# The first keys' inverse root moved to VectorE, two GpSimd steps held behind the key product at the start, and a new table of due times

## The chip, the cores and the metric

One core of one Trainium2 chip runs one program. The metric is the device time of one execution in microseconds (us); a smaller time is better. The program has five instruction streams that run side by side and wait for each other by semaphores: PE (TensorE, matrix products and transposes), ACT (ScalarE), DVE (VectorE), POOL (GpSimd) and SP (SyncE, which here issues every DMA transfer). Each stream executes its instructions strictly in the order in which the program gives them.

## The reference

Attention over 8 batches of 12 heads with 448 positions of width 64, followed by a two-layer network on the 3584 resulting rows of width 768. All tensors are 32-bit floats on the device; the weights can come in as 64-bit numbers that the kernel decodes.

```python
def rmsnorm(x, g):
    rms = np.sqrt(np.mean(x * x, axis=-1, keepdims=True) + 1e-06)
    return x / rms * g
q_n, k_n = (rmsnorm(q, g_q), rmsnorm(k, g_k))
scores = scale * np.matmul(q_n, k_n.transpose(0, 1, 3, 2))
scores = scores - np.max(scores, axis=-1, keepdims=True)
attn = np.exp(scores)
attn = attn / (np.sum(attn, axis=-1, keepdims=True) + 1e-09)
attn_out = np.matmul(attn, v).astype(np.float32)
x = np.ascontiguousarray(attn_out.transpose(0, 2, 1, 3)).reshape(B * S, H * D)
h = x @ w_in              # 768 -> 2048
g = h * np.cos(h)
return (g @ w_out).astype(np.float32)   # 2048 -> 768
```

## The kernel before

**Units and batches.** Two heads make a unit, so there are 48 units (u), six to a batch. `prepare(u)` loads and normalizes a unit's queries and keys, `attend(u)` computes its scores, exponentials and products with v. The six units of the first batch are "plain": their products run on full 32-bit operands (`score_plain` L533, `av_plain` L660 to L670). From the seventh unit on, every operand is split into a high and a low part of a shorter format and the product is made from parts (`score` L549, `av` L642 and L644).

**The first keys.** For units 0 and 1 the keys come in rows with one position per partition. ACT squares them (`kn_square` L399), DVE sums the squares (`kn_reduce` L405), POOL adds a constant and takes the power -0.5 (`kn_pow` L409, L410), DVE multiplies the keys by the result (`kn_norm` L415), PE turns them (`kn_turn` L420) and ACT copies the turned keys with the gains (`kn_copy` L425). For unit 0 all but `kn_pow` go in two halves. Then PE's first scores begin (L533).

**The inverse roots for the softmax.** For every unit, ACT squares queries and keys in another layout (`st_square` L372), DVE sums (`st_reduce` L375), POOL takes the power (`st_pow` L380, L381). `rowmin` (L553, DVE) multiplies a tile of scores by these values and finds the extreme of each row; `expo` (L561, ACT) is the exponential.

**The keys of units 2 to 5.** Their inverse roots go through memory: `st_store` (L428) writes them out, `rk_spread` (L433) reads them back spread over the partitions (tile D), `k_load` (L448) loads the keys into the one key buffer kq, and POOL multiplies the two in two instructions (`k_norm` L458, tile km), the product that lets PE's scores of the unit begin. `k_load` of the next unit can be issued only when `k_norm` has read the buffer.

**Other work of POOL at the start.** `x_norm` (L699) multiplies a finished unit's attention output by its inverse sums. `w_low` (L267) makes the low part of a decoded weight tile, in two halves; the decoded tile lies in one of two buffers (wf, aq) that DVE's `w_decode` (L244 to L252) fills again afterwards. `q_scale` (L474) scales the queries.

**The order of the work.** No stream decides anything while it runs. Before, the class `Plan` lays out the whole program: every piece of work is added with its engine, an assumed cost, a due time, what it reads and what it writes. `order()` then plays the program through: of the pieces that could start on an engine it takes the one with the smallest due time, and the sequence in which pieces were taken is the order in which the instructions are written out. The due times are formulas of the unit plus a shift from the table `SHIFT`. A shift has three columns: for later units (u of 9 and up, later batches), for units 6 to 8 (for the two-layer network: the first batch), and for units 0 to 5.

**After the head.** The first product of the network for a batch (`ffn1` L726 to L728, `h_out` L744) is mixed into the attention of the next batch; the probabilities are transposed on PE (`transp` L595, L600, L604), copied out as high part (`pt_high` L618, ACT) and low part (`pt_low` L625 and L627, DVE). From about 890 us on only the network is left; its second product is `ffn2` (L800 to L802).

Of the kernel before, what the change touches and what calls it, by code (L numbers as in the profile page):

```python
# [10 lines left out]
F32 = mybir.dt.float32  # L11
F32R = mybir.dt.float32r
I32 = mybir.dt.int32
AF = mybir.ActivationFunctionType
ALU = mybir.AluOpType
# [5 lines left out]
PE, ACT, DVE, POOL, SP = "PE", "ACT", "DVE", "POOL", "SP"  # L21


class Plan:
# [46 lines left out]
    def order(self):  # L71
# [26 lines left out]
        seq = []  # L98
# [3 lines left out]
        while True:  # L102
            best = None
            for e in free:
                if can[e]:
                    t = free[e]
                elif wait[e]:
                    t = max(free[e], wait[e][0][0])
# [6 lines left out]
            t, e = best  # L115
            while wait[e] and wait[e][0][0] <= t:
                n = heapq.heappop(wait[e])[1]
                heapq.heappush(can[e], (parts[n][2], n))
            n = heapq.heappop(can[e])[1]
            cost, fn, args, kb = (parts[n][i] for i in (1, 3, 4, 6))  # L120
# [21 lines left out]
                    heapq.heappush(wait[parts[m][0]], (ready[m], m))  # L142
        assert len(seq) == len(parts)
        self.end = dict(free)
        self.seq = seq
        return [(fn, args) for _, _, fn, args in seq]


@with_exitstack
def tile_attention_moe(  # L150
# [11 lines left out]
    nc = tc.nc  # L162
    NU = sd_in.shape[0]
    B, S, D = 8, kq_in.shape[2] - 512, 64
# [11 lines left out]
    KB = S // 4  # L176
# [32 lines left out]
    def g_fold():  # L209
# [5 lines left out]
    wts, wfl, raw = {}, {}, {}  # L215
    RING = {
# [3 lines left out]
    }  # L220

# [94 lines left out]
    pair = {}  # L316
# [37 lines left out]
    def tl(u, name, shape, dt, tag=None):  # L354
        tag = tag or name
        t = pair.setdefault(u, {})[name] = apool.tile(shape, dt, tag=tag, name=f"{name}{u}", bufs=RING[tag])
        return t
# [28 lines left out]
    def kn_bank(u):  # L386
        return pt[u]
# [13 lines left out]
    def kn_reduce(u, a, b):  # L401
        if a == 0:
            tl(u, "rn", [128, 8], F32)
        sq = kn_bank(u)[:KB, 128 * a : 128 * b].rearrange("p (t d) -> p t d", d=D)
        nc.vector.tensor_reduce(pair[u]["rn"][:KB, 2 * a : 2 * b], sq, axis=AX.X, op=ALU.add)  # L405

    def kn_pow(u):
        r = pair[u]["rn"][:KB]
# [266 lines left out]
    xf = {}  # L675
# [141 lines left out]
    def y_store(b, oc, src):  # L817
# [2 lines left out]

    plan = Plan(RING, loose=PKEYS)
    SHIFT = {
        "av": (5.3, 0.0, 0.0), "av3": (3.6, 0.0, 0.0), "av_plain": (0.0, 0.0, 15.8), "e_place": (-4.5, 0.0, 0.0),
        "expo": (8.1, 0.0, 0.0), "ffn1": (0.0, -3.8, 0.0), "h_out": (-4.4, 0.0, 0.0), "k_high": (5.2, 7.1, 0.0),
        "kq_load": (-19.1, 0.0, 0.0), "m_place": (15.1, -13.5, 0.0), "pt_copy0": (0.0, 0.0, -3.9),
        "pt_high1": (-1.8, 0.0, 0.0), "pt_low0": (-20.7, 9.3, 0.0), "pt_low1": (-5.9, 0.0, 0.0),
        "q_high": (5.1, 0.0, 0.0), "q_low": (-2.0, 3.7, 0.0), "q_scale": (-9.4, -8.6, 0.0),
        "rowmin": (10.1, 6.2, 1.1), "rs_copy": (0.0, 2.2, 0.0), "rs_load": (0.0, 0.0, -12.0),
        "rs_store": (6.6, 0.0, 11.5), "rsum": (-8.3, 0.0, 0.0), "st_pow": (-14.6, 0.0, 0.0),
        "st_reduce": (5.3, 0.0, 0.0), "st_square": (2.5, 0.0, 0.0), "transp0": (-4.1, 0.0, 0.0),  # L830
        "transp1": (2.4, -8.7, 0.0), "v_decode": (8.3, 0.0, 0.0), "v_high": (0.0, 12.8, 0.0),
        "v_load": (19.8, -12.8, 0.0), "v_store": (12.5, 0.0, 0.0), "w_decode": (0.4, 0.0, 0.0),
        "x_norm": (4.0, 0.0, 0.0), "x_plain": (0.0, 0.0, -20.3), "x_split": (-3.4, 0.0, 0.0),
        "x_sum": (13.2, 0.0, 0.0),
    }

    def add(eng, cost, due, fn, *args, **more):
        name, first = fn.__name__, args[0] if args else 0
        stage = 0
        if name in ("ffn1", "h_out", "h_store", "h_both", "x_split"):  # L840
            stage = int(first < (NP if name == "x_split" else 1))
        elif name[:2] not in ("w_", "v_", "e_") or name in ("v_load", "v_high", "v_low", "v_plain", "e_place"):
            stage = 2 if first < NP else int(first < NP + 3)
        if name in ("pt_low", "pt_high", "pt_copy", "transp"):
            name += str(args[2])
        elif name == "av" and args[1] == 3:
            name += "3"
        due += SHIFT.get(name, (0.0,) * 3)[stage]
        if name in ("w_load", "w_decode", "w_high", "w_low"):
            due += -0.414 * first  # L850
        if name in ("ffn1", "h_out", "h_store", "h_both") and not first:
            due += -0.355 * args[1]
        if name in ("v_fetch", "v_decode", "v_sum", "v_split", "v_store"):
            due += 25.441 * first
        cost *= {DVE: 1.059, ACT: 1.026, POOL: 1.021}.get(eng, 1.0)
        plan.add(eng, cost, due, fn, *args, **more)
# [68 lines left out]
    def prepare(u):  # L925
        D0 = base(u)
        kmw = [km_key(u)]
        sd, r, kd, khi, qd, qhi = ([(n, u)] for n in ("sd", "r", "kd", "khi", "qd", "qhi"))
        sd = [("sd", max(u, NKT - 1), u)]
        turned, plain = u < NKT, u < NP  # L930
        if turned:
            kn, rn, kb = [("qd" if u == 0 else "ql", u)], [("rn", u)], [("pt", 0, n) for n in ((0,) if u == 0 else (1, 2))]
            add(SP, ISS, D0 - 60, kn_load, u, w=kn, kb=224.0)
            halves = ((0, 2), (2, 4)) if u == 0 else ((0, 4),)
            hs = [("kn", u, h) for h in halves]
            sh = 1.0 / len(halves)
            for h, k in zip(halves, hs):
                add(ACT, 0.06 + 0.57 * sh, D0 - 50, kn_square, u, *h, r=kn, w=[k, *(kb if h[0] == 0 else [])])
            for h, k in zip(halves, hs):
                add(DVE, 0.06 + 0.63 * sh, D0 - 50, kn_reduce, u, *h, r=[k, *kb], w=[("rn" if h[0] == 0 else "rm", u)])  # L940
            add(POOL, 1.9, D0 - 50, kn_pow, u, r=kb, w=rn + [("rm", u)])
            for h, k in zip(halves, hs):
                add(DVE, 0.06 + 0.63 * sh, D0 - 50, kn_norm, u, *h, r=rn + kn, w=[k])
            for h, k in zip(halves, hs):
                add(PE, 0.98 * sh, D0 - 50, kn_turn, u, *h, r=[k, *kn, *kb], w=[k])
            for n, (h, k) in enumerate(zip(halves, hs)):
                add(ACT, 0.73 if u else (0.36, 0.53)[n], D0 - 50, kn_copy, u, *h, r=[k, *kb, ("gsc", 0)], w=kmw)
        elif plain:
            add(SP, ISS, D0 - 36, k_load, u, w=kd, kb=224.0, start=D0 - 36)
        else:  # L950
            add(SP, ISS, D0 - 34, kq_load, u, w=kd + qd, kb=480.0, start=D0 - 40)
# [162 lines left out]
    for u in range(NP):  # L1114
        prepare(u)
# [28 lines left out]
    add = plan.add  # L1144
# [3 lines left out]
    for fc in range(NEAR, NFC):  # L1148
        n = fc - NEAR
        d, y, he = BLOCK * n, ("y", n % 8), (("he", "he2")[n % 2], n // 2)  # L1150
# [32 lines left out]
    for t in range(B // 2):  # L1183
# [26 lines left out]
        for k, (name, q, w0, bk, opens, closes) in enumerate(PRODUCTS):  # L1210
# [6 lines left out]
            for g in range(NGR):  # L1217
                n, n_split = n_split, n_split + 1
# [5 lines left out]
                for o in range(3):  # L1224
                    add(PE, BLOCK / 3, e + BLOCK / 3 * o, ffn2, n, g, wpos, role[bk][o], o, opens,
                        r=[hk, lk] + [("wp", i) for i in wpos], w=[("y", role[bk][o])])
# [8 lines left out]
            for o in range(3):  # L1235
                y, s0 = ("y", role[bk][o]), 4 * o
# [78 lines left out]
```

## Time and profile before

| what | value |
|---|---|
| median of 3 runs | 1373.23 us (1372.65 to 1375.12) |
| the profiled execution's own time | 1371.8 us |
| its span, first to last instruction | 1370.0 us |
| busy share PE, DVE, ACT, POOL | 98%, 78%, 68%, 46% |
| instructions in the span | 21500 |
| DMA | 302.19 MB, mean 221 GB/s |

The profile shows one execution. A line number (L458) is a line of the kernel, "km<-kq,D" says that tile km is written from kq and D, and a time is counted from the span's start. The busy share is an average over stages with different limits, so it is read together with the waits of each stretch: an engine's idle time before an instruction and what ended it. [...]

### The profile page before, as it was taken

Reading aid. Unit: us, or ns where it says so; the run is one execution under the profiler, and the core shown is the slowest. Engines: PE = TensorE matmul, PEld = TensorE weight load, DVE = VectorE, ACT = ScalarE, POOL = GpSimd, SP = SyncE. Lnnn points to the kernel's source line nnn. Section 1 sums busy time; section 2 is a strip of 40 time slices with the busy share of each in tenths; the row PEclk is TensorE's granted clock in tenths of the full one; section 3 lists DMA queues with packets and bytes.
Section 4 is the critical chain, followed back from the end, with each engine's and each line's share of the span. In section 5 each row is a group of like instructions: output and inputs, shape, how many; then the busy total and the mean of one; then the engine's idle time right before and its main releaser. Section 6 shows DMA issues by size and latency. Waiting matters only on the chain.

```text
span 1370.0 us, 21500 instructions
## 1 busy us (share of the span) xinstructions
PE 1343.2 (98%) x6998; PEld 1171.0 (85%) x6998; DVE 1075.0 (78%) x1859; ACT 927.4 (68%) x1872; POOL 632.5 (46%) x554
## 2 busy tenths in 40 slices
PE   7899999999999999999999999999999999999998
PEld 3346888788888989888889888999999999999998
DVE  7888899977787887787877877628889889889742
ACT  6677878777877877777777787638666366366321
POOL 4889978676766866666776584330000000000000
PEclk9999999999999999999999999999999999999999
DMA  6798776889798899798987897338988369369334
GB/s 241 263 276 194 186 170 188 240 232 244 201 260 212 216 243 209 218 243 227 247 209 196 227 233 200 120 131 315 370 298 300 119 246 306 112 247 313 105 113 153
DMA packets 149472, 302.19 MB, mean 221 GB/s; under 512 B 34368, under 2 KB 83088, under 8 KB 149360
## 3 DMA queue, kind: packets, MB, share of 16 engines
q1 hardware_dynamic: 149360, 300.83, 75.2%
q8 instruction: 55, 0.90, 0.3%
q14 instruction: 57, 0.47, 0.1%
HBM read 193.99 MB, written 62.73 MB: 187 GB/s over the span
## 4 chain that ended last, share of the span: by engine, by line
PE 86%; POOL 5%; DVE 3%; DMA 2%; issue 2%; ACT 1%; SPq 0%; POOLq 0%; ACTq 0%; DVEq 0%
PE y L800 10%; PE y L802 10%; PE y L801 10%; PE ph L726 9%; PE ph L727 8%; PE ph L728 8%; PE S L549 8%; PE PT L595 7%; PE O L642 4%; PE O L644 3%; PE O L660 1%; PE S L533 1%; PE y L727 1%; PE y L728 1%; PE y L726 1%
## 5 line engine op out<-in xcount | busy, mean ns | idle before, releaser
L553 DVE TENSOR_SCALAR_CACHE_REDUCE S<-S,r 128x448 f32<-128x448 f32 x336 | 225.3, 686 | 56.4 <-PE S L549 45.4
L561 ACT ACTIVATE P<-S,sm 128x448 f32<-128x448 f32 x336 | 213.3, 637 | 73.8 <-DVE S L553 56.7
L726 PE MATMUL ph<-xs,wi 128*128 128x448 f32 x660 | 251.1, 380 | 1.6 <-ACT hbuf L744 1.6
L800 PE MATMUL y<-g,wo 128*128 128x448 f32 x672 | 245.4, 365 | 0.0
L801 PE MATMUL y<-g,wo 128*128 128x448 f32 x672 | 245.4, 365 | 0.0
L802 PE MATMUL y<-g,wo 128*128 128x448 f32 x672 | 245.4, 365 | 0.0
L727 PE MATMUL ph<-xs,wi 128*128 128x448 f32 x660 | 241.7, 366 | 0.0
L728 PE MATMUL ph<-xs,wi 128*128 128x448 f32 x660 | 241.3, 366 | 0.0
L782 ACT CAST g<-gq 128x896 fp32r<-128x896 f32 x112 | 105.7, 944 | 170.6 <-PE y L802 170.1
L618 ACT CAST hi<-PT 128x512 fp32r<-128x512 f32 (+2 forms) x336 | 175.7, 532 | 63.7 <-PE PT L595 23.8
L625 DVE TENSOR_TENSOR lo<-PT,hi 128x512 fp32r<-128x512 f32 (+1 forms) x252 | 153.2, 619 | 41.2 <-ACT hi L618 39.0
L780 DVE TENSOR_TENSOR g<-gq,g 128x896 fp32r<-128x896 f32 x112 | 122.0, 1089 | 60.2 <-ACT g L782 59.7
L595 PEld LDWEIGHTS PT<-ident,P 128*128 128x128 f32 x1008 | 124.0, 141 | 42.2 <-issue 6.6
L595 PE MATMUL PT<-ident,P 128*128 128x128 f32 x1008 | 155.8, 275 | 2.8 <-DVE rt L574 1.2
L726 PEld LDWEIGHTS ph<-xs,wi 128*128 128x128 f32 x660 | 124.2, 188 | 17.8 <-ACT hbuf L744 3.4
L800 PEld LDWEIGHTS y<-g,wo 128*128 128x128 f32 x672 | 126.2, 188 | 10.0
L802 PEld LDWEIGHTS y<-g,wo 128*128 128x128 f32 x672 | 126.2, 188 | 9.9
L801 PEld LDWEIGHTS y<-g,wo 128*128 128x128 f32 x672 | 126.2, 188 | 9.9
L728 PEld LDWEIGHTS ph<-xs,wi 128*128 128x128 f32 x660 | 124.0, 188 | 10.6
L727 PEld LDWEIGHTS ph<-xs,wi 128*128 128x128 f32 x660 | 124.4, 189 | 8.6
L381 POOL TENSOR_TENSOR r<-r,nhalf 128x14 f32<-128x14 f32 (+1 forms) x48 | 124.5, 2593 | 4.0
L642 PE MATMUL O<-hi,vs 128*128 128x448 f32 x336 | 122.3, 378 | 1.1 <-DVE hi L627 0.8
(129 smaller groups left out, 2635.9 us busy)
## 6 DMA issues: line engine op xcount, KB each, us to landing
wo<-wo_d SPq DMA_DIRECT2D x152, 384.0 KB
gq<-h_d SPq DMA_DIRECT2D x64, 448.0 KB
h_d<-hbuf SPq DMA_DIRECT2D x54, 448.0 KB
wo_d<-ao SPq DMA_DIRECT2D x56, 384.0 KB
sd<-sd SPq DMA_DIRECT2D x46, 448.0 KB
kq<-kq SPq DMA_DIRECT2D x42, 480.0 KB
D<-qhi SPq DMA_DIRECT2D x84, 192.0 KB
raw<-w_in SPq DMA_DIRECT2D x16, 768.0 KB
```

The source lines that it names most:

```text
L553: nc.vector.tensor_scalar(d["S", t][:, :S], d["S", t][:, :S], d["r"][:, t : t + 1], None, op0=ALU.mult, op1=ALU.min, accum_out=d["sm"][:, ...
L561: nc.scalar.activation(p_rows(u, t), d.pop(("S", t))[:, :S], AF.Exp, bias=sm[:, 1, t : t + 1], scale=-1.0, accum_out=sm[:, 2, t : t + 1],)
L595: nc.tensor.transpose(pt[part][:, i * 128 : i * 128 + 128], p_rows(u, t)[:, c : c + 128], ident)
L618: nc.scalar.copy(hi if kc < 3 else hi[:64], pt_rows(u, kc, part))
L625: nc.vector.tensor_tensor(lo, src, hi.bitcast(F32), ALU.subtract)
L642: nc.tensor.matmul(O, st, d["hi", kc][:, HEADS[hh]], start=(kc == 0), stop=(kc == 3))
L726: nc.tensor.matmul(ph[:, :S], whi, x2[:, 0, :], start=(cc == 0), stop=False)
L727: nc.tensor.matmul(ph[:, :S], whi, x2[:, 1, :], start=False, stop=False)
L728: nc.tensor.matmul(ph[:, :S], wlo, x2[:, 0, :], start=False, stop=(cc == NCC - 1))
L800: nc.tensor.matmul(y, whi, hi[:, e], start=first and e == 0, stop=False, **more)
L801: nc.tensor.matmul(y, whi, lo[:, e], start=False, stop=False, **more)
L802: nc.tensor.matmul(y, wlo, hi[:, e], start=False, stop=last and e == NG - 1, **more)
```

## The change

Four edits:

- `kn_root` is new. For unit 0 alone it takes the place of `kn_pow`: the inverse root is computed on DVE from a bit-pattern estimate and three rounds of Newton's method, twelve instructions on 112 x 8 numbers. Unit 1 keeps `kn_pow`. The planner is told a cost of 0.85 us for it (1.9 us for `kn_pow`).
- `hold` is new in `Plan`. After the sequence is made, it goes through it once: an `x_norm` or `w_low` whose planned time lies before 60 us is taken out if a `k_norm` that stands behind it in the sequence has a planned time less than 4 us later, and is put back right behind the next `k_norm`. Nothing else moves.
- Six shifts in the table of due times become zero: `e_place` (-4.5, later units), `pt_low` of the first half (-20.7, later units), `transp` of the second half (-8.7, units 6 to 8), `q_low` (3.7, units 6 to 8), `ffn1` (-3.8, first batch), `rowmin` (1.1, units 0 to 5).
- Two small tiles for `kn_root` are added (ry, rt8).

```diff
-        self.seq = seq
+        self.seq = seq = self.hold(seq)
...
+    YIELD, AHEAD, WITHIN, UNTIL = ("x_norm", "w_low"), "k_norm", 4.0, 60.0
+
+    def hold(self, seq):
+        out, held = [], []
+        for i, item in enumerate(seq):
+            t, n, fn, args = item
+            name = fn.__name__
+            if name in self.YIELD and t < self.UNTIL and any(
+                f.__name__ == self.AHEAD for s, _, f, _ in seq[i:] if s < t + self.WITHIN
+            ):
+                held.append(item)
+                continue
+            out.append(item)
+            if name == self.AHEAD:
+                out += held
+                held = []
+        assert not held
+        return out
...
+    def kn_root(u):
+        x = pair[u]["rn"][:KB]
+        y, t = (tl(u, name, [128, 8], F32)[:KB] for name in ("ry", "rt8"))
+        nc.vector.tensor_scalar(x, x, D * 1e-6, 3.0e38, op0=ALU.add, op1=ALU.min)
+        nc.vector.tensor_scalar(
+            y.bitcast(I32), x.bitcast(I32), 1, 0x7FFFFFFF, op0=ALU.logical_shift_right, op1=ALU.bitwise_and
+        )
+        nc.vector.tensor_scalar(y.bitcast(I32), y.bitcast(I32), -1.0, 1597463007.0, op0=ALU.mult, op1=ALU.add)
+        for last in (False, False, True):
+            nc.vector.tensor_tensor(t, x, y, ALU.mult)
+            nc.vector.scalar_tensor_tensor(t, t, -0.5, y, op0=ALU.mult, op1=ALU.mult)
+            nc.vector.scalar_tensor_tensor(x if last else y, t, 1.5, y, op0=ALU.add, op1=ALU.mult)
...
-        "pt_low0": (-20.7, 9.3, 0.0), "pt_low1": (-5.9, 0.0, 0.0),
+        "pt_low0": (0.0, 9.3, 0.0), "pt_low1": (-5.9, 0.0, 0.0),
...
-            add(POOL, 1.9, D0 - 50, kn_pow, u, r=kb, w=rn + [("rm", u)])
+            if u:
+                add(POOL, 1.9, D0 - 50, kn_pow, u, r=kb, w=rn + [("rm", u)])
+            else:
+                add(DVE, 0.85, D0 - 50, kn_root, u, r=kb, w=rn + [("rm", u)])
```

## Rows read from the trace of the kernel before

**Rows 1.** The profile's first page: busy time of each engine, share of the span, number of instructions.

```profile
PE 1343.2 (98%) x6998; PEld 1171.0 (85%) x6998; DVE 1075.0 (78%) x1859; ACT 927.4 (68%) x1872; POOL 632.5 (46%) x554
```

**Rows 2.** Busy time by stretches of 150 us: stretch, its length, busy time of each engine with its instructions, granted clock, DMA share, GB/s.

```profile
0.00:150.00 150.00, 132.15 (x591) 74.90 (x592) 127.38 (x261) 110.50 (x253) 119.69 (x105) 0.99 0.82 237
...
300.00:450.00 150.00, 150.00 (x835) 134.68 (x835) 118.64 (x254) 116.80 (x275) 103.59 (x93) 1.00 0.85 229
```

**Rows 3.** Waits of PE from 0 to 60 us: who waited for whom, us in total, times, longest.

```profile
PE PT L420 <- DVE kq L415: 7.7, 1, 7.7
PE S L533 <- POOL km L458: 3.5, 2, 1.8
```

**Rows 4.** Waits of PE from 60 to 300 us, the four largest of nine.

```profile
PE S L549 <- ACT P L561: 2.3, 4, 1.0
PE ph L726 <- ACT hbuf L744: 1.4, 1, 1.4
PE PT L595 <- DVE rt L574: 1.2, 1, 1.2
PE O L644 <- DVE lo L625: 1.0, 1, 1.0
```

**Rows 5.** Waits of PE from 300 to 1360 us, the largest of three.

```profile
PE PT L595 <- DVE lo L625: 0.7, 3, 0.3
```

**Rows 6.** The timeline from 3 to 12.2 us, all engines, the rows of the first keys and of the first softmax values: start, duration, engine, line, operation, tiles, shapes, count, and in brackets the idle time before it and what ended it.

```profile
4.30 0.75 DVE L405 TENSOR_REDUCE rn<-PT 112x4 f32<-112x256 f32 x2 [0.51 <-ACT PT L399]
...
5.43 1.66 POOL L410 TENSOR_TENSOR rn<-rn,nhalf 112x8 f32<-112x8 f32 x1
...
6.69 0.62 DVE L375 TENSOR_REDUCE r<-sd 128x7 f32<-128x448 f32 x1 [1.63 <-ACT sd L372]
7.23 0.75 DVE L415 TENSOR_TENSOR kq<-kq,rn 112x256 f32<-112x256 f32 x2
...
7.80 1.53 POOL L381 TENSOR_TENSOR r<-r,nhalf 128x7 f32<-128x7 f32 x1
...
9.65 3.35 PE L533 MATMUL S<-kn,q 64*128 64x448 f32 x7 [0.93 <-ACT kn L425]
9.70 1.63 POOL L410 TENSOR_TENSOR rn<-rn,nhalf 112x8 f32<-112x8 f32 x1
...
11.65 0.69 DVE L553 TENSOR_SCALAR_CACHE_REDUCE S<-S,r 128x448 f32<-128x448 f32 x1 [2.42 <-POOL r L380]
```

**Rows 7.** Small instructions of DVE (timeline, and for the reciprocal the groups from 300 to 900 us, with count, busy us and mean ns), and two instructions of which the second reads what the first wrote.

```profile
0.79 0.06 DVE L202 MEMSET nhalf<- 128x1 f32 x1 [0.79 <-PEq L1305]
...
3.63 0.16 DVE L210 SCALAR_TENSOR_TENSOR gs<-gs 128x2 f32<-128x2 f32 x1 [2.75 <-DMA gs<-gg]
...
L571 DVE RECIPROCAL sm<-sm 128x7 f32<-128x7 f32 x31 | 6.1, 198 | 11.6 <-ACT sm L569 11.3
...
36.16 0.54 DVE L244 TENSOR_SCALAR wf<-raw 128x768 int32<-128x768 int32 x1
36.74 0.96 DVE L246 SCALAR_TENSOR_TENSOR wf<-raw,wf 128x768 int32<-128x768 int32 x1
```

**Rows 8.** The timeline of POOL from 38 to 51 us.

```profile
37.99 1.71 POOL L699 TENSOR_TENSOR xf<-xf,rs 128x448 f32<-128x448 f32 x1
39.66 0.99 POOL L267 TENSOR_TENSOR wi<-aq,wi 128x384 fp32r<-128x384 f32 x1
40.62 2.24 POOL L458 TENSOR_TENSOR km<-kq,D 128x448 f32<-128x448 f32 x2
...
45.95 2.59 POOL L381 TENSOR_TENSOR r<-r,nhalf 128x14 f32<-128x14 f32 x1
48.51 0.99 POOL L267 TENSOR_TENSOR wi<-wf,wi 128x384 fp32r<-128x384 f32 x1
49.45 2.12 POOL L458 TENSOR_TENSOR km<-kq,D 128x448 f32<-128x448 f32 x2
```

**Rows 9.** Line L458 alone, from 30 to 45 and from 45 to 56 us: the sequencer of POOL waiting on behalf of `k_norm` for its transfers (ns min/median/max, then first and last start in us). The sequencer runs ahead of the engine.

```profile
L458 POOLq EVENT_SEMAPHORE  x1: 577/577/577, 36.5 to 36.5; - x1
...
L458 POOLq EVENT_SEMAPHORE  x1: 43/43/43, 48.3 to 48.3; - x1
```

**Rows 10.** The timeline of PE from 39 to 53 us.

```profile
39.09 1.72 PE L660 MATMUL O<-hi,vs 128*64 128x448 f32 x4
42.51 2.16 PE L533 MATMUL S<-km,q 64*128 64x448 f32 x8 [1.71 <-POOL km L458]
...
50.64 2.37 PE L533 MATMUL S<-km,q 64*128 64x448 f32 x4 [1.84 <-POOL km L458]
```

**Rows 11.** The timeline of SP's queue from 38 to 52 us: the issue of the next keys' load and of the queries' load.

```profile
42.88 0.33 SPq L448 DMA_DIRECT2D kq<-kq  x1
...
49.42 0.42 SPq L470 DMA_DIRECT2D q<-kq  x1
```

**Rows 12.** The timeline of POOL from 57 to 64 us.

```profile
56.98 0.69 POOL L474 TENSOR_SCALAR q<-q,gs 128x512 f32<-128x512 f32 x1 [3.80 <-DMA q<-kq]
...
61.19 2.78 POOL L458 TENSOR_TENSOR km<-kq,D 128x448 f32<-128x448 f32 x2
```

**Rows 13.** The chain of waits that ended last, in order of time, one piece: start, us, what.

```profile
63.02 2.02 PE S L533 x6
```

**Rows 14.** Busy time and granted clock in one short stretch, columns as in rows 2.

```profile
52.16:55.58 3.42, 3.42 (x13) 1.86 (x11) 3.00 (x7) 2.63 (x6) 1.02 (x1) 0.50 0.80 315
```

More of the change, by code (lines that the diff above doesn't have):

```diff
@@ L822, in tile_attention_moe @@
     SHIFT = {
[L823 to L834, printed above, removed]
+        "av": (5.3, 0.0, 0.0), "av3": (3.6, 0.0, 0.0), "av_plain": (0.0, 0.0, 15.8), "expo": (8.1, 0.0, 0.0),
+        "h_out": (-4.4, 0.0, 0.0), "k_high": (5.2, 7.1, 0.0), "kq_load": (-19.1, 0.0, 0.0),
+        "m_place": (15.1, -13.5, 0.0), "pt_copy0": (0.0, 0.0, -3.9), "pt_high1": (-1.8, 0.0, 0.0),
+        "pt_low0": (0.0, 9.3, 0.0), "pt_low1": (-5.9, 0.0, 0.0), "q_high": (5.1, 0.0, 0.0),
+        "q_low": (-2.0, 0.0, 0.0), "q_scale": (-9.4, -8.6, 0.0), "rowmin": (10.1, 6.2, 0.0),
+        "rs_copy": (0.0, 2.2, 0.0), "rs_load": (0.0, 0.0, -12.0), "rs_store": (6.6, 0.0, 11.5),
+        "rsum": (-8.3, 0.0, 0.0), "st_pow": (-14.6, 0.0, 0.0), "st_reduce": (5.3, 0.0, 0.0),
+        "st_square": (2.5, 0.0, 0.0), "transp0": (-4.1, 0.0, 0.0), "transp1": (2.4, 0.0, 0.0),
+        "v_decode": (8.3, 0.0, 0.0), "v_high": (0.0, 12.8, 0.0), "v_load": (19.8, -12.8, 0.0),
+        "v_store": (12.5, 0.0, 0.0), "w_decode": (0.4, 0.0, 0.0), "x_norm": (4.0, 0.0, 0.0),
+        "x_plain": (0.0, 0.0, -20.3), "x_split": (-3.4, 0.0, 0.0), "x_sum": (13.2, 0.0, 0.0),
     }
```

2 rows, old and new, of the table RING are left out of this document.

## The prediction

> **What bounds the kernel now.** I read the busy shares first: TensorE is busy for 1343.2 of 1370.0 us, no other engine for over 78% [rows 1]. An average says little here, so the table by stretches came next: from 300 us on PE is busy for the whole stretch, while in the first 150 us it is busy for 132.15 [rows 2]. What can still be won without taking work from PE therefore lies ahead of 300 us, and PE's waits say where. From 0 to 60 us it stands 7.7 us until the first keys are normed, and 3.5 us, in two pieces, for POOL's key product L458 [rows 3]. From 60 to 300 us the four largest waits sum to 2.3 + 1.4 + 1.2 + 1.0 = 5.9 us, on ACT's exponentials, an eviction, DVE's small copy and DVE's low parts [rows 4]. From 300 us to the end the largest is 0.7 us in three pieces [rows 5]. So the reader should see a kernel with some 3.5 us to win in the head at L458, some 6 us between 60 and 300 us, and almost nothing afterwards, where a new order can only lose.
>
> **Part 1, the inverse root of the first keys on DVE.** Removed: POOL's constant and power. From the end of the sums (4.30 + 0.75 = 5.05) to the first norming (7.23) pass 2.18 us; the power ends at 5.43 + 1.66 = 7.09, and DVE meanwhile does the sum of squares of the softmax values at 6.69 [rows 6]. Added: 3 + 3 x 3 = 12 DVE instructions, each reading what the one before it wrote. The trace has no such chain of small ones, so I bound it. A small instruction with tensor operands takes 0.16 us (L210); a memory set of one column takes 0.06, a reciprocal of seven columns 0.20. A dependent instruction begins 0.04 us after the end of the one that it reads: 36.16 + 0.54 = 36.70 against 36.74 [rows 7]. So 12 x (0.16 + 0.04) = 2.4 us, between 12 x 0.10 = 1.2 and 12 x 0.24 = 2.9. I take 2.4, since L210 is one of the very instructions used. Norming then begins at 5.05 + 2.4 = 7.45 and not 7.23: +0.2 us on the path to the first scores at 9.65, from -1.0 to +0.7.
>
> [...]
>
> Moved by it: the sum of squares at 6.69 now stands behind root and norming, at about 7.45 + 0.75 = 8.2. Its power then ends 1.5 us later, at 7.80 + 1.53 + 1.5 = 10.8, still ahead of the first `rowmin` at 11.65 [rows 6]: cost 0. Unit 1's power (9.70 + 1.63 = 11.3) ends near 12.8; its norming on DVE could then wait, with rowmins behind it. I take 0, with up to 0.5 us. POOL's freed 1.9 us are worth nothing: its next piece waits for DVE's sum anyway.
>
> **Part 2, GpSimd's order.** Before unit 2's key product stand an `x_norm` from 37.99 and a `w_low` from 39.66; the product starts at 40.62 [rows 8]. Its transfers had landed: the sequencer's wait for them ended at 36.5 + 0.58 = 37.1 [rows 9]. With both held, the product starts at 38.0, 2.6 us sooner. PE ran out of work at 39.09 + 1.72 = 40.81 and stood 1.71 us until 42.51 [rows 10]; that wait goes, -1.7 us. What is late next is unit 3. Its transfers landed at 48.3 + 0.04 [rows 9], and ahead of its product (49.45) stand a power from 45.95 and a `w_low` of 0.99 [rows 8]. The two held pieces still run between the two products, so the power keeps its place; only the 0.95 us from 48.51 to 49.45 go. PE's scores of unit 3 then start near 50.64 - 1.0 and no sooner, after a wait that is longer by 0.7 [rows 10]. Of 3.5 us of waits, 1.0 is a real gain at 50 us.
>
> Does it stay? Unit 4's product starts at 61.19, ends at 63.97, and PE's scores of it are due just then [rows 12, 13]: it has no slack. POOL stood 3.80 us before it, for a load of queries [rows 12] issued at 49.42. SP issues in order, and stood at unit 3's key load until 42.88, the end of unit 2's product [rows 8, 11]. That end comes 2.6 us sooner, so the transfers behind it do too, and I take unit 4 to move by the 1.0 needed. If not, the gain ends there. The held pieces cost nothing on POOL; a held `w_low` keeps its weight buffer 2 us longer, which only meets DVE's next decode (up to 0.5 us).
>
> **Part 3, the due times.** They take no work away; they reorder. The four that concern units 0 to 8 and the first batch act where PE still waits: 5.9 us in the four groups [rows 4], the most that they can give. The two for later units act where PE waits for a low part for 0.7 us in all [rows 5]; there they can give nothing, and lose. Nothing in the trace tells how the new order falls out, so my value is 0, bounds -6 and +5 (the price of the slower rival below).
>
> **The sum.** +0.2 - 1.0 + 0 = -0.8 against a profiled execution of 1371.8 us (span 1370.0), 0.1% below the median of 1373.23. I apply the difference to the median: 1372.4 us. About 0.2%, 2.7 us, is what a measurement of this kernel can tell from no change.
>
> **The rivals.**
> *Due times that win.* Half to all of the waits between 60 and 300 us go [rows 4]: -3 to -6 more, and PE may keep its clock. [...] For it: part 2 shortens what PE stood in all before 50 us by 1.0. Against it: the wait just ahead of unit 3 grows. Price: -0.8 - 4 = -4.8, 1368.4 us; with the clock 1366.7.
> *Low parts behind rowmins, the slower side.* For 39 later units the first half's low part loses a lead of 20.7 in due time. DVE can then put a `rowmin` (0.69 us [rows 6]) ahead of it, and PE's products with it wait. For it: the largest wait of PE from 300 us on is just this one [rows 5]. Against it: three such waits in all say that the low parts have cover. 39 units have 117 such low parts; if 7 lose their cover by one rowmin, 7 x 0.69 = 4.8 us, and with -0.8 the time is 1377.2. It decides from five such waits on (3.5 - 0.8 = 2.7).
> *The head's gain is absorbed.* Unit 4's product does not move (its load of queries lands when it did), PE waits there for the 1.0 us it had won, and DVE's chain costs 0.2 to 0.7: 1373.4 to 1373.9. For it: no slack at 63.97 [rows 12, 13]. Against it: SP's early issue.
> *The root does what its planned cost says*, 0.85 us: norming starts 1.3 us sooner, 1370.9 in place of 1372.4. For it only the memory set's 0.06 us.
>
> **How the numbers follow.** My forecast holds with 0.40, own range 1370.6 to 1374.3 (root from -1.0 to +0.7, small losses up to 1). Due times that win: 0.27. Slower by low parts: 0.18. Absorbed: 0.11. Root as planned: 0.04. Faster by over 0.2% is nearly all of the second (0.26) and the low tail of the first and the last (0.05): 0.31. Slower is nearly all of the third (0.16) and the high tail of the first (0.03): 0.19. The rest, 0.50, lies within 0.2%. The range of 1367 to 1377.5 leaves out the second rival with the clock and the third beyond seven waits, about 0.2 together.
>
> **What would show it.** On DVE, twelve rows between the sums near 5.05 and the first norming, near 0.2 us from start to start; PE's first transposes near 7.9 and not 7.7 [rows 3]. On POOL, L458 at 38.0 and 48.5, each followed by what had stood ahead of it. On PE, no wait at 42.5, one of about 2.5 us before 49.6, and unit 4's scores near 63. In the waits of 60 to 300 us a sum other than today's tells of the due times, and any wait over a microsecond behind L625 after 300 us of the slower rival. I am wrong if the head's stretch to 64 us is not about 1 us shorter, or if PE's waits behind it change by more than 2 us.

## The result and the profile after

The changed kernel takes 1384.29 us (median of 5 runs, 1380.89 to 1390.65) against 1373.23 us of the kernel before (5 runs beside it, 1371.64 to 1376.4): ratio 1.0086, 95% interval 1.0068 to 1.0103. It is slower by some 11 us, where I had forecast 0.8 us faster; the time lies outside the range and on the other side. The profiled execution is the longest of the five, 1390.65 us, span 1388.9. Three executions in the runs below took 3419 to 5627 us in place of some 1380, and no ratio contains them, nor does the median of the root alone.

The busy shares barely move, so they don't tell where the time went. PE's busy time grows by 13.2 us with the same 6998 instructions [rows 1]:

```profile
PE 1356.4 (98%) x6998; PEld 1173.4 (84%) x6998; DVE 1086.4 (78%) x1871; ACT 927.7 (67%) x1872; POOL 633.7 (46%) x552
```

The same table by stretches, with two of the second layer added (columns as in [rows 2], the engines in the order PE, PEld for PE's weight loads, DVE, ACT, POOL):

```profile
0.00:150.00 150.00, 130.64 (x571) 72.74 (x572) 125.77 (x263) 105.56 (x241) 111.93 (x98) 0.94 0.81 232
300.00:450.00 150.00, 147.84 (x818) 131.49 (x817) 121.66 (x252) 113.23 (x268) 103.40 (x89) 1.00 0.85 228
900.00:1050.00 150.00, 150.00 (x727) 136.23 (x727) 109.23 (x116) 89.62 (x119) 13.30 (x12) 1.00 0.77 278
1050.00:1200.00 150.00, 150.00 (x728) 136.22 (x727) 129.35 (x134) 83.78 (x96) 0.00 (x0) 1.00 0.63 217
```

The first row has 571 instructions of PE where there were 591, at a mean granted clock of 0.94 (before 0.99). The last two rows hold the surprise: PE is busy for the whole stretch at a granted clock of 1.00 and still does only 727 and 728 instructions. The kernel before does this in both stretches:

```profile
900.00:1050.00 150.00, 150.00 (x742) 139.04 (x741) 110.41 (x113) 91.93 (x115) 6.26 (x6) 1.00 0.81 289
1050.00:1200.00 150.00, 150.00 (x742) 139.04 (x741) 127.48 (x133) 78.88 (x90) 0.00 (x0) 1.00 0.60 208
```

From start to start, 128x448 products follow each other every 202.67 ns in the kernel before and every 206.67 ns in the changed one. I call this the pitch. It shows in the page too, as 368 ns a product where the kernel before has 365 (the row of the kernel before first):

```profile
L800 PE MATMUL y<-g,wo 128*128 128x448 f32 x672 | 245.4, 365 | 0.0
L832 PE MATMUL y<-g,wo 128*128 128x448 f32 x672 | 247.3, 368 | 0.0
```

To see where the 19 us of the two profiled executions come from, I subtracted the starts of the same products: +0.5 us at the first scores, +4.8 at 89 us, +7 at 301 us, +10 from 359 to 890 us, then +1 until 957 us and +8 in the second layer (2016 products x 4.0 ns), where nothing waits. So there are three places: the head, PE's waits at 258 and 316 us, and the pitch.

**The head.** The timeline of the chain in DVE, and what follows (as [rows 6]):

```profile
4.38 0.76 DVE L424 TENSOR_REDUCE rn<-PT 112x4 f32<-112x256 f32 x2 [0.51 <-ACT PT L418]
...
5.17 0.17 DVE L429 TENSOR_SCALAR rn<-rn 112x8 f32<-112x8 f32 x1
...
5.37 0.17 DVE L430 TENSOR_SCALAR ry<-rn 112x8 int32<-112x8 int32 x1
...
7.38 0.17 DVE L437 SCALAR_TENSOR_TENSOR rn<-rt,ry 112x8 f32<-112x8 f32 x1
7.58 0.76 DVE L447 TENSOR_TENSOR kq<-kq,rn 112x256 f32<-112x256 f32 x2
...
9.51 1.66 POOL L442 TENSOR_TENSOR rn<-rn,nhalf 112x8 f32<-112x8 f32 x1
...
11.25 0.21 POOL L399 TENSOR_SCALAR r<-r 128x7 f32<-128x7 f32 x1
11.55 1.49 POOL L400 TENSOR_TENSOR r<-r,nhalf 128x7 f32<-128x7 f32 x1
11.62 0.68 DVE L447 TENSOR_TENSOR kn<-kn,rn 112x512 f32<-112x512 f32 x1
...
13.07 0.69 DVE L585 TENSOR_SCALAR_CACHE_REDUCE S<-S,r 128x448 f32<-128x448 f32 x1 [0.77 <-POOL r L400]
```

The chain is as worked out: twelve instructions 0.20 us apart, 2.4 us from 5.17 to the norming at 7.58. But the order behind it is another. On POOL unit 1's key power (9.51) now stands ahead of unit 0's softmax power (11.55, before 7.80), so the first `rowmin` starts at 13.07 and not 11.65. On ACT the copy of unit 1's keys stands ahead of the first exponential (15.23; before 12.44), and PE waits for that (the row of the kernel before first, then two of the changed one):

```profile
12.44 0.63 ACT L561 ACTIVATE P<-S,sm 128x448 f32<-128x448 f32 x1 [2.50 <-DVE S L553]
```

```profile
14.25 0.96 ACT L457 ACTIVATE kn<-PT,gs 128x448 f32<-128x448 f32 x2 [3.20 <-PE PT L452]
15.23 0.63 ACT L593 ACTIVATE P<-S,sm 128x448 f32<-128x448 f32 x1
```

```profile
16.01 3.40 PE L565 MATMUL S<-kn,q 64*128 64x448 f32 x5 [1.80 <-ACT P L593]
```

Behind this wait the granted clock is 0.50 for 6.83 us; two more such stretches stand around the wait ahead of unit 3's scores and behind the one at 258 us (20.5 us in all, 3.4 before [rows 14]):

```profile
16.78:23.61 6.83, 6.83 (x18) 2.63 (x17) 4.63 (x12) 3.41 (x11) 0.00 (x0) 0.50 0.22 84
50.91:61.15 10.24, 6.98 (x19) 3.08 (x18) 7.77 (x17) 5.73 (x14) 6.92 (x6) 0.50 1.00 309
259.13:262.54 3.41, 3.41 (x13) 2.93 (x12) 2.64 (x7) 1.61 (x5) 1.01 (x1) 0.50 0.73 204
```

These stretches aren't counted as a cause of their own. A kernel among the experiments below that loses nothing (the two due times for later units, profiled execution 1372.79 us) has 13.65 us at 0.50 from 43.53 us on and a mean granted clock of 0.994, beside the changed kernel's 0.993 and 0.999 before; and the root alone, with a mean of 0.996, loses 4.0 us by 20 us (the whole change 4.5) without any such stretch near 17 us.

**The hold**, on POOL and on PE (as [rows 8, 10]):

```profile
39.11 3.37 POOL L400 TENSOR_TENSOR r<-r,nhalf 128x14 f32<-128x14 f32 x1
42.45 2.82 POOL L490 TENSOR_TENSOR km<-kq,D 128x448 f32<-128x448 f32 x2
...
50.60 3.28 POOL L400 TENSOR_TENSOR r<-r,nhalf 128x14 f32<-128x14 f32 x1
53.85 1.66 POOL L490 TENSOR_TENSOR km<-kq,D 128x448 f32<-128x448 f32 x2
```

```profile
45.19 1.89 PE L565 MATMUL S<-km,q 64*128 64x448 f32 x8
...
55.17 2.25 PE L565 MATMUL S<-km,q 64*128 64x448 f32 x4 [3.26 <-POOL km L490]
```

Unit 2's product follows its power at once and PE's wait of 1.71 us is gone; in front of unit 3's scores PE waits 3.26 us instead of 1.84.

**The due times.** Of PE's waits beyond 60 us, two that have grown are shown [rows 4, 5]: DVE's small copy from 1.2 to 2.2 us, and beyond 300 us a transposition behind a low part from 0.7 us in three pieces to 1.5 us in one (the wait for `h_out` grew there too, from 0.2 to 1.3 us):

```profile
PE PT L627 <- DVE rt L606: 2.2, 1, 2.2
```

```profile
PE PT L627 <- DVE lo L657: 1.5, 1, 1.5
```

### The profile page after: what moved, and what is told of

It is laid out like the page before. It is cut to its first block, busy times and chain, and to the rows that moved or that the text cites. A ratio compares the mean times of both kernels' runs of the same rounds, so it can differ in the third digit from the quotient of the medians.

```text
span 1388.9 us, 21523 instructions
## 1 busy us (share of the span) xinstructions
PE 1356.4 (98%) x6998; PEld 1173.4 (84%) x6998; DVE 1086.4 (78%) x1871; ACT 927.7 (67%) x1872; POOL 633.7 (46%) x552
## 4 chain that ended last, share of the span: by engine, by line
PE 85%; DVE 5%; DMA 3%; POOL 3%; ACT 2%; issue 2%; SPq 0%; POOLq 0%; ACTq 0%; DVEq 0%
PE y L834 10%; PE y L832 10%; PE y L833 10%; PE ph L758 8%; PE ph L759 8%; PE ph L760 8%; PE S L581 7%; PE PT L627 7%; PE O L674 4%; PE O L676 3%; PE S L565 2%; PE O L692 1%; DMA h_d<-hbuf 1%; PE y L759 1%; PE y L758 1%
```

## The experiments

Each kernel is the one before with one part of the change, unless said otherwise, timed beside the kernel before. That took 1373.7 us beside the root, the hold, the due times and the changed kernel; 1374.14 beside the root in the old order, the whole change with another price and the two groups of due times; 1374.07 beside the hold for unit 2 and the three runs that separate chain and tiles; 1374.74 and 1374.7 in the last six. The edits are shown in part: of the table of due times only the entries that differ, put together on one line, and without what goes along with a line (the functions `kn_root`, `hold` and `kn_idle`, the entries of the new tiles). Where an edit is against another kernel than the one before, the text says which.

**The parts, one by one.** The runs of the root, of the hold, of the due times and of the changed kernel set two theories against each other: H, that the low price lets the plan put unit 1's keys ahead of unit 0's softmax, which costs 4 to 6 us, and that the due times cost the rest; and D, that the new due times alone make the loss. The root alone, at its planned cost of 0.85:

```diff
-            add(POOL, 1.9, D0 - 50, kn_pow, u, r=kb, w=rn + [("rm", u)])
+            if u:
+                add(POOL, 1.9, D0 - 50, kn_pow, u, r=kb, w=rn + [("rm", u)])
+            else:
+                add(DVE, 0.85, D0 - 50, kn_root, u, r=kb, w=rn + [("rm", u)])
```

> The kernel before with the inverse root on VectorE alone, priced 0.85 us in the plan. [...] Theory D (the new due times alone make the loss): within 1 us of the kernel before.

1387.6 us (1384.58 to 1388.58), ratio 1.0094 (1.0079 to 1.0109): slower than the whole change beside it (1.006, below). Its order differs from that of the kernel before in the first 15 us only, and PE's not at all. Its profiled execution loses 4.0 us by 20 us, some 2.5 more by 150 us, nothing from there to 890 us, and 9.4 us afterwards by the pitch of 206.67 ns (727 instructions of PE from 900 to 1050 us, 742 before). The 2.5 us are not told from scatter: the five kernels below that add only unused tiles, and so keep the order, differ from the kernel before by -0.2 to 1.2 us at 20 us and by -0.6 to 4.2 us at 170 us.

The hold alone:

```diff
+        self.seq = seq = self.hold(seq)
```

> The kernel before with the two GpSimd steps held behind the key product alone. My forecast: the key product of unit 2 at 38.0 and of unit 3 at 48.5, PE's wait at 42.5 gone, 1 us faster (0 to 2.7). [...]

1373.48 us, ratio 0.9997 (0.9988 to 1.0005): no gain. At 43 us it has won 1.8 us, at unit 3's scores nothing is left:

```profile
47.78 3.28 POOL L400 TENSOR_TENSOR r<-r,nhalf 128x14 f32<-128x14 f32 x1
51.03 1.66 POOL L477 TENSOR_TENSOR km<-kq,D 128x448 f32<-128x448 f32 x2
```

The power starts 1.83 us later than in the kernel before (45.95 [rows 8]), an offset that this execution had before (PE's products of 39.09 [rows 10] start at 40.72). The `w_low` of 0.99 us between power and product is gone, but the power takes 3.28 instead of 2.59 us. The hold brings this: in the five profiles with the hold on the order of the table it took 3.28 us here, in the fourteen without the hold 2.59. (The one more with the hold, with the root at 2.3, has another order there and 2.59.) The product comes 0.25 us sooner, not 0.95.

The hold for unit 2 alone, where the `w_low` stays ahead of unit 3's product:

```diff
-    YIELD, AHEAD, WITHIN, UNTIL = ("x_norm", "w_low"), "k_norm", 4.0, 60.0
+    YIELD, AHEAD, WITHIN, UNTIL = ("x_norm", "w_low"), "k_norm", 4.0, 45.0
```

> The kernel before with GpSimd's norming of x and low weights held for the third key tile alone; the fourth key tile's queue is as before. If the product of the fourth key tile waited longer with the hold on both only because its own queue was changed, the 1.6 us gained at 43 us stay: 1371.5 to 1373 us, ratio 0.9985 to 0.9995. If the time gained is slack that the fourth key tile's product, which waits for GpSimd's own chain (power, store, spread, norming), takes back anyway: 1373 to 1375 us, ratio 0.9995 to 1.001, and a PE wait of about 3.5 us instead of 1.84 us before it.

```profile
46.00 3.28 POOL L400 TENSOR_TENSOR r<-r,nhalf 128x14 f32<-128x14 f32 x1
49.25 1.14 POOL L286 TENSOR_TENSOR wi<-wf,wi 128x384 fp32r<-128x384 f32 x1
50.34 1.73 POOL L477 TENSOR_TENSOR km<-kq,D 128x448 f32<-128x448 f32 x2
```

```profile
51.53 2.45 PE L552 MATMUL S<-km,q 64*128 64x448 f32 x4 [4.65 <-POOL km L477]
```

1375.48 us, ratio 1.0013 (1.0004 to 1.0022). Here the power starts when it did before (46.00, 45.95), takes 0.69 us more, and the product comes 0.9 us later (50.34, 49.45 [rows 8]); PE waits 4.65 us in one piece where it waited 1.71 and 1.84.

The six due times alone:

```diff
-        "transp1": (2.4, -8.7, 0.0), "q_low": (-2.0, 3.7, 0.0), "rowmin": (10.1, 6.2, 1.1), "ffn1": (0.0, -3.8, 0.0)
+        "transp1": (2.4, 0.0, 0.0), "q_low": (-2.0, 0.0, 0.0), "rowmin": (10.1, 6.2, 0.0), "ffn1": (0.0, 0.0, 0.0)
-        "pt_low0": (-20.7, 9.3, 0.0), "e_place": (-4.5, 0.0, 0.0)
+        "pt_low0": (0.0, 9.3, 0.0), "e_place": (0.0, 0.0, 0.0)
```

> The kernel before with the six shifts at zero alone. Theory H: nothing lost up to 100 us, 3 to 6 us lost between 170 and 340 us, so 3 to 6 us slower. Theory D: 9 to 11 us slower. If the shifts do nothing by themselves: within 1 us.

1380.22 us, ratio 1.0055 (1.0033 to 1.0077). In its profiled execution it is +1.9 us at 170 us, +3.1 at 340 (waits of 2.18 and 1.13 us where the whole change has 2.18 and 1.47), then new waits in the second layer, +6.7 at the end. Its runs spread from 1376.59 to 1387.79 us.

The changed kernel again:

> The changed kernel once more, beside the others on one chip. Both theories: ratio near 1.0086, 9 to 13 us slower. If the 2% slower rate of its network stage in the first profile belongs to the kernel, that stage is again 8 us longer than in the kernel before; if it belongs to that execution, it is not.

1383.14 us (1378.93 to 1383.4), ratio 1.006 (1.0048 to 1.0072). Its profiled execution, 1378.93 us, tells the most: the pitch is slow until 963.7 us, where two products start 250 and 310 ns behind the ones ahead of them, and fast from there on. PE's instructions in two stretches of 60 us:

```profile
900.00:960.00 60.00, 60.00 (x293) 54.49 (x292) 25.93 (x28) 31.10 (x46) 11.62 (x11) 1.00 0.57 205
1010.00:1070.00 60.00, 60.00 (x298) 55.61 (x297) 54.10 (x57) 42.66 (x49) 0.00 (x0) 1.00 0.89 318
```

So the pitch can change within one execution, and the changed kernel's runs spread over 11.7 us (1378.93 to 1390.65) where the pitch of the second layer is worth 8.

**The price of the root.** The chain on DVE, planned as POOL's power was, so that the order is the old one (against the root alone):

```diff
-                add(DVE, 0.85, D0 - 50, kn_root, u, r=kb, w=rn + [("rm", u)])
+                add(POOL, 1.9, D0 - 50, kn_root, u, r=kb, w=rn + [("rm", u)])
```

> The kernel before with the inverse root on VectorE, but planned as the GpSimd power was planned, so that every other instruction keeps its place. Theory H (the order made from the low price costs, not the twelve instructions): unit 1's keys stay behind unit 0's softmax, first rowmin within 0.6 us of 11.65, PE at 20 us within 1 us of the kernel before, and the whole within 1.5 us of it. Rival R (the chain of twelve instructions on VectorE itself costs): PE at 20 us again some 4 us late, 6 us slower or more.

1383.81 us, ratio 1.0076 (1.0064 to 1.0088). In the head this loses only 1.0 us by 20 us and 1.4 to 2.1 until 889 us, and PE's wait of 1.80 us is not there. So some 3 of the 4 us of the head come from the order that the price 0.85 made. The other 9.4 us are the slow pitch again (727 instructions of PE from 900 to 1050 us), though PE's order is that of the kernel before.

The whole change with a price near the measured one (against the changed kernel):

```diff
-                add(DVE, 0.85, D0 - 50, kn_root, u, r=kb, w=rn + [("rm", u)])
+                add(DVE, 2.3, D0 - 50, kn_root, u, r=kb, w=rn + [("rm", u)])
```

> The changed kernel with the root priced 2.3 us in the plan, near what its twelve instructions took (2.4 us). Theory H: unit 0's power and exponentials go ahead of unit 1's again, PE at 20 us within 1.5 us of the kernel before, and 3 to 5 us faster than the changed kernel, so 4 to 6 us slower than the kernel before (what the due times cost). Rival R: no faster than the changed kernel.

1386.49 us, ratio 1.0088 (1.0073 to 1.0103). The start is mended (+0.4 us at 20), but the new order puts a wait elsewhere, and nothing is won:

```profile
PE S L565 <- ACT P L593: 6.2, 1, 6.2
```

**Which due times.** The four that concern units 0 to 8 and the first batch, and the two for later units:

```diff
+        "transp1": (2.4, 0.0, 0.0), "q_low": (-2.0, 0.0, 0.0), "rowmin": (10.1, 6.2, 0.0), "ffn1": (0.0, 0.0, 0.0)
```

> The kernel before with the four shifts at zero that concern units 0 to 8 and the first batch. Theory L (the two shifts of later units make the loss): within 1.5 us of the kernel before, GpSimd's weight parts and the last store of them near 921 us as before. Theory E (the four make it): 3 to 6.5 us slower, the last store 10 us late.

1381.1 us, ratio 1.0051 (1.0035 to 1.0066): all of the loss. Nothing is lost up to 170 us; from 359 us on it is some +3, and +6.3 at the end. What is added comes in the second layer, where the kernel before never waits:

```profile
PE y L800 <- DMA wo<-wo_d: 1.4, 1, 1.4
PE y L800 <- DVE outs L813: 0.8, 1, 0.8
```

The two for later units:

```diff
+        "pt_low0": (0.0, 9.3, 0.0), "e_place": (0.0, 0.0, 0.0)
```

> The kernel before with the two shifts at zero that concern later units (the low part's lead of 20.7 and that of e_place). Theory L: 4 to 6.5 us slower, a wait of PE for a low part near 310 us, the last store of the weight parts near 932 us instead of 921 and PE waiting 1 to 4 us for loads between 960 and 1000 us. Theory E: within 1.5 us of the kernel before, none of these.

1374.86 us, ratio 1.0006 (0.9998 to 1.0015): no difference that can be told.

**Where the pitch comes from.** By now four kernels had begun the network with the slow pitch, each with `kn_root`, and five with the fast one, each without. Three things go with the function: its instructions, their time, and two small tiles. First the old order with the chain's temporaries in a free slot of the buffer P (against the root in the old order):

```diff
-        y, t = (tl(u, name, [128, 8], F32)[:KB] for name in ("ry", "rt8"))
+        y, t = (pbuf[:KB, 8, c : c + 8] for c in (0, 8))
```

> The kernel before with the inverse root on VectorE in the old order, as in the run of the old order (1383.81 us), but the chain's two temporaries lie in a slot of the weights' buffer P that is still unused at 5 us, so that no new tile stands among the others and no address moves. All three theories are about the pitch of the network's products from 893 us on, 206.67 ns in every kernel with the chain and 202.67 ns in every kernel without it, some 8 us. Theory A (the two small tiles move by 64 bytes per partition what is allocated behind them): pitch 202.67 ns, 1374 to 1376 us. Theory I (twelve more instructions in VectorE's stream, wherever they write): 206.67 ns, 1382 to 1385 us. Theory T (the third of a microsecond by which the first norming comes later, carried to the end as a phase): 206.67 ns, 1382 to 1385 us.

1375.31 us, ratio 1.0006 (0.9997 to 1.0015), fast pitch. Then the tiles without the chain (against the kernel before):

```diff
             tl(u, "rn", [128, 8], F32)
+            if u == 0:
+                tl(u, "ry", [128, 8], F32), tl(u, "rt8", [128, 8], F32)
```

> The kernel before, the power on GpSimd, with nothing but the two small tiles added, unused: no instruction more, the tiles allocated behind them 64 bytes per partition further on. A: pitch 206.67 ns, 1381 to 1384 us. I and T: 202.67 ns, 1372 to 1375 us.

1384.33 us (1381.46 to 1385.26), ratio 1.0069 (1.0055 to 1.0083), slow pitch from 894 us to the end. Not one instruction was added, and the order and the waits are those of the kernel before. The two stretches, first with the chain and without the tiles, then with the tiles and without the chain:

```profile
900.00:1050.00 150.00, 150.00 (x742) 139.04 (x741) 108.56 (x112) 92.73 (x117) 8.50 (x8) 1.00 0.80 285
```

```profile
900.00:1050.00 150.00, 150.00 (x728) 136.24 (x727) 106.69 (x109) 91.04 (x116) 8.97 (x8) 1.00 0.78 278
```

The twelve instructions as idle work on a free slot of P (`kn_idle`), beside POOL's power:

```diff
     def kn_pow(u):
         r = pair[u]["rn"][:KB]
+        if u == 0:
+            kn_idle()
```

> The kernel before, the power on GpSimd and used as before, and beside it the same twelve VectorE instructions on numbers that nobody reads, in a slot of the weights' buffer that is unused at 5 us. No tile more. I: pitch 206.67 ns, 1381 to 1384 us. A: 202.67 ns, 1372 to 1375 us. T: the norming waits for the later of the two, about 7.5 instead of 7.2 us, so 206.67 ns if that third of a microsecond is what decides.

1374.64 us, ratio 1.0008 (0.9999 to 1.0017), fast pitch. So it is the tiles: they move the tiles allocated behind them by 64 bytes per partition, r, vs, sm, wf, hi and the rest. The operands of the network's products (xs, wi) don't move. How the changed kernel does without this move (against the changed kernel):

```diff
-        y, t = (tl(u, name, [128, 8], F32)[:KB] for name in ("ry", "rt8"))
+        y, t = (pbuf[:KB, 8, c : c + 8] for c in (0, 8))
```

> The changed kernel whole (chain at its low price, hold, six shifts zero), with the chain's two temporaries in a slot of the weights' buffer that is unused at 5 us, so that no tile moves. Theory A (the move alone makes the slow pitch): pitch 202.67 ns from 893 us on, and what stays are the order of the head and the due times, +5 to +7 us against the kernel before: 1378 to 1381 us, ratio 1.003 to 1.005. Rival (the due times or the order of the head make it too): 206.67 ns, 1383 us or more.

1381.83 us, ratio 1.0055 (1.0041 to 1.0069). Neither theory fits whole: the network begins at the fast pitch, as the move predicts (298 instructions of PE from 900 to 960 us), but behind a wait of 1.05 us at 999 us it is slow to the end in the profiled execution (292 from 1010 to 1070 us), the longest of six (1378.83 to 1389.46). The due times alone bring a wait there too.

Which tiles count, with an unused tile of 64 bytes ahead of hi, ahead of rt and ahead of sm, and one of 32 bytes in the first place:

```diff
+                apool.tile([128, 16], F32, tag="pad", name="pad", bufs=1)
```

> The kernel before with one unused tile of 64 bytes per partition ahead of the high parts of the weights (hi): these and what lies behind them move, the values vs stay. Theory M (the place of hi, the moving operand of the last attention products before the network): 206.67 ns, 1381 to 1385 us. Theory V (the place of vs, the stationary operand): 202.67 ns, 1372 to 1376 us. Theory Q (tiles behind hi: the parts of queries and keys, x): 206.67 ns.

> The kernel before with the unused tile of 64 bytes behind hi: the parts of queries and keys, x and the row sums move, vs and hi stay. M and V: 202.67 ns, 1372 to 1376 us. Q: 206.67 ns, 1381 to 1385 us.

> The kernel before with the unused tile of 64 bytes per partition behind the values vs and ahead of the row sums sm: sm, wf, hi and all behind them move, r and vs stay. Theory V (the place of the values, the stationary operand of the attention's last products, or of r): pitch 202.67 ns from 893 us on, 1371 to 1375 us. Theory W (sm or wf): 206.67 ns, 1381 to 1385 us.

> The kernel before with one unused tile of 32 bytes per partition in the place of the chain's two: everything that these moved by 64 bytes moves by 32. If any move of these tiles ends the fast pitch: 206.67 ns, 1381 to 1385 us. If the place counts only in steps of 64 bytes or only decides by chance how the last products fall: either pitch, 202.67 ns with 1372 to 1376 us as likely as the other.

1372.92, 1373.56, 1374.22 and 1372.28 us, ratios 0.9993, 0.9993, 1.0003 and 0.9993 (all intervals within 0.9981 to 1.0014): all fast. Of the places tried, only the 64 bytes ahead of r and vs bring the slow pitch; 32 bytes there don't. vs is the stationary operand of the attention's last products, the last thing that PE does before the network runs alone; that points to it, but it could be r, and why 64 bytes and not 32 stays open.

Last, the kernel with the two unused tiles, and a small transposition ahead of every fourth block of the first layer that runs alone (against the kernel with the two tiles):

```diff
     def ffn1_block(b, fc, bank):
+        knocked.append(fc)
+        if len(knocked) % 4 == 1:
+            nc.tensor.transpose(banks[bank][:7, S : S + 64], ident[:64, 0:7], ident[:64, :64])
```

> The kernel with the two unused tiles, whose pitch was 206.67 ns from 893 us to the end (1384.33 us), with one small transposition more (7 x 64, into unused columns of the product's bank) ahead of every fourth block of network products that run alone, at most 0.1 us each. Theory L (the pitch is kept by products without a break and drawn anew by any break): the pitch changes at one of these places at least, and what it is at the last of them it keeps through the second layer; with the fast one 1374 to 1378 us, with the slow one 1381 to 1385 us. Theory P (the places of the tiles hold the pitch through the stage): 206.67 ns throughout, 1383 to 1386 us.

1374.12 us (1372.57 to 1378.23), ratio 1.0002 (0.9992 to 1.0012), in place of 1384.33. The timeline of PE, at the first of them:

```profile
912.64 0.37 PE L728 MATMUL S<-xs,wi 128*128 128x448 f32 x1
912.85 0.37 PE L729 MATMUL S<-xs,wi 128*128 128x448 f32 x1
913.06 0.37 PE L730 MATMUL S<-xs,wi 128*128 128x448 f32 x1
913.35 0.22 PE L737 MATMUL y<-ident 64*7 64x64 f32 x1
913.50 0.47 PE L728 MATMUL y<-xs,wi 128*128 128x448 f32 x1
913.81 0.37 PE L729 MATMUL y<-xs,wi 128*128 128x448 f32 x1
914.02 0.36 PE L730 MATMUL y<-xs,wi 128*128 128x448 f32 x1
```

Up to 913.06 the products are 368 ns long in the mean, from 914 us on 365, to the end of the kernel; two more transpositions leave it so. The first one puts the two products behind it back by some 0.34 us (913.06 to 913.81, where three starts at the slow pitch lie 0.41 us apart), not by the 0.1 us that I expected. The tiles are where they were. So the place of the tiles doesn't hold the pitch here: with these tiles the run began with 368 ns a product, and behind the transposition it went on with 365.

## Why the prediction was wrong

**Part 1, the chain: right.** I said 12 x (0.16 + 0.04) = 2.4 us; it is 12 x 0.20, 0.17 us an instruction and 0.03 us between two. The first transposes came at 8.26 in this execution, where I had said 7.9: 0.09 us of it is a later end of the sums, and from the norming to the transposes pass 0.68 us where it was 0.51. Without the tiles and in the old order the chain costs 1.2 us by the medians, which is not told from nothing (ratio 1.0006, 0.9997 to 1.0015). In that order DVE does the sum of squares between the chain and the norming, which starts at 7.88 there and not at my 7.45.

**Part 1, what it moves: wrong.** The step that failed is "Unit 1's power ... I take 0, with up to 0.5 us". I kept the order of the trace and moved the times in it. The order is made anew by the planner, with 0.85 us for a chain of 2.4; it put unit 1's power ahead of unit 0's softmax power, and the first `rowmin` came at 13.07 in place of 11.65. The root alone is 4.0 us late at 20 us in the new order and 1.05 us in the old, so the order costs some 3 us there. In the whole times this is not clear of noise: the ratios are 1.0094 and 1.0076, and their intervals overlap. That my rival "the root does what its planned cost says" asked only for the chain's duration missed that the cost acts on the order whether or not it is true.

**Part 2: the first half right, "1.0 is a real gain" wrong.** Product 2 starts behind its power and PE's wait goes, as said. The term that failed is the 0.95 us at unit 3: the power ahead of it grew by 0.69 us, so the gain there is 0.25, and in the whole time nothing (0.9997). With unit 2 alone held the product even came 0.9 us later. What PE wins at unit 2 it waits at unit 3, because POOL does the same pieces in between and unit 3's power does not start sooner for it.

**Part 3: the value of 0 wrong, and the slower rival misplaced.** The upper bound of +5 was passed (+7.0 for the four alone). I looked for the loss where the low parts of later units would lose their cover; those two shifts cost nothing (1.0006). It came from the four that I took for the ones that could win, because I priced them by the waits that they could remove (5.9 us) and not by those that they make: +3 us by 359 us and 2.2 us of waits in the second layer, where there had been none. The 1.7 us by which the price of the faster rival falls "with the clock", to 1366.7, are shown by no run: the changed kernel has 20.5 us at a granted clock of 0.50 where there were 3.4, so nothing was given back, and the two due times for later units, at a mean granted clock of 0.994, took 1374.86 us, no different from the kernel before (1.0006).

**Not in the sum at all: the tiles.** This is the step that failed most. I put the "two small tiles" at nothing without a reason. They cost 10.3 us alone (1384.33 - 1374.07, ratio 1.0069), nearly the whole loss, and 9.4 us of it show as the slow pitch of the products from 894 us on, a stretch of which I had said only that a new order can lose there.

The parts don't add up: 10.3 for the tiles, some 3 for the order, 7.0 for the due times and up to 1.2 for the chain make 21.5 us, while the whole costs 11.1 and, measured again, 9.4. Part of it is shown: the slow pitch and the due times' waits in the second layer are not independent, since a break there can end the slow pitch (the changed kernel's second profile) or start it (a wait in the same without the tiles). How the rest overlaps was not separated.

## What to carry to other kernels

A planned cost is part of the change: with a new price the whole order ahead is a new one, and has to be made and read before anything is summed on the old timeline. A queue's product moved forward by itself won nothing here (ratio 0.9997, and 1.0013 with unit 2 alone), since the piece that the next product waits for did not start sooner (unit 3's power at 46.00 us, 45.95 before). And before a change is judged, its pitch of equal products in a long stretch without waits is to be compared (instructions of PE per stretch at full busy share): here two unused tiles of 32 bytes per partition cost 10.3 us, over ten times what I had forecast of all edits, and a small transposition, a break of some 0.34 us, took it back (1374.12 us in place of 1384.33).

## What was unexpected in the hardware

- Equal 128x448 products on PE at the same granted clock of 1.00 ran at one of two pitches, 202.67 or 206.67 ns from start to start, for hundreds of microseconds without a wait. In these runs the pitch with which the products began stayed to the end or changed at a break: a pause of 0.15 us at 964 us in the changed kernel's second profile (slow to fast), a wait of 1.05 us at 999 us in the same without the tiles (fast to slow), a 7 x 64 transposition (slow to fast). Not every break changed it: the four due times' waits of 1.4 and 0.8 us in the second layer left the fast one. Why there are two was not found. 2016 products x 4.0 ns are 8 us.
- The pitch at the start of the run changed here with the place of tiles that none of its products reads: 64 bytes ahead of r and vs brought the slow one (1384.33 us), 32 bytes there (1372.28), or 64 bytes behind vs (1372.92 to 1374.22), the fast one.
- POOL's power over 128x14 numbers takes 2.58 or 2.59 us in 41 of 46 instructions of the kernel before and 2.87 to 3.37 in the other five (in the changed kernel 38, and eight with 2.69 to 3.37): unit 3's took 3.28 us in five profiles with the hold and 2.59 in the fourteen without. What it meets there was not tried.
